# Fused set attention and gated convolution: token groups of 508 that carry their own halo, h summed over units on VectorE, and a last batch with float16 output products and a value product in two halves

## The chip, the core and the metric

The kernel runs on one core of one Trainium2 chip. The metric is the device time of one execution in microseconds; smaller is better. A core has TensorE (PE in the profile; PEld is its loading of weights), VectorE (DVE), ScalarE (ACT), GpSimd (POOL) and SyncE (SP), and 16 DMA engines that move data between main memory and the core's own.

## What is computed

For each of 4 batches, x holds 12800 tokens of 128 channels, and 32 inducing vectors of 128 channels are shared. The first attention makes h (32 by 128) from all tokens of the batch, the second attends from each token to h, and the result goes through a causal convolution over 5 tokens that gates a product with w_val, and a product with w_out:

```python
def mab(q, kv):
    s = scale * (q @ kv.transpose(0, 2, 1))
    a = softmax(s)
    return a @ kv
h = mab(inducing, x)
y = mab(x, h)
gate_pre[t] = sum(conv_w[k] * y[t - 4 + k] for k in range(5))
out = (sigmoid(gate_pre) * (y @ w_val)) @ w_out
```

h for a batch needs every token of that batch, so a batch has two stages with a short serial step between them.

## The kernel before

The tokens of a batch are cut into 7 **units**: 6 big ones of 4 groups with 512 tokens each, and a small one of 4 groups with 128 (`units`). The 4 groups of a unit lie in the 4 strips of 32 partitions, so that 32 score rows for each of 4 groups fill 128 partitions.

**Loads.** Each unit is loaded twice from main memory by SP's queue: `load_t` (L218) brings channels on partitions into tile xT (12 buffers), and `load_k` (L223) brings tokens on partitions into tile xk (4 buffers). The host lays xk out so that 128 consecutive tokens are the 128 rows of one block; a big unit has 16 blocks, and so 128 rows of 8 KB. SP issues the loads of all units in order, each xT followed by its xk, and waits at a load until its buffer is free.

**Stage 1**, per unit: scores in `a_mm` (L236), maximum in `a_max`, exponential in `a_exp`, transposes by PE in `a_tr` (L252), their copy in `a_ev`, and `a_h` (L265), which multiplies by xk and sums the unit's share of h; `a_hev` (L271) copies it to hs.

**Between the stages**, per batch: the functions `p_nl` to `p_we`. They find the maximum over the units and each unit's factor f, sum the 7 shares of h on PE (`p_h`, L321: 7 float32 products with a diagonal F made in `p_F`), and make the weights of stage 2: hq for the scores, and float16 high and low parts of the convolution and value weights (wstk). wo is w_out with a scale (L367).

**Stage 2**, per unit: scores `b_mm` (L389) from xT again, which is the last use of an xT buffer; a softmax in `b_tr` to `b_back`; float16 high and low parts in `b_hi` (L432, ACT) and `b_lo` (L437, POOL). The convolution needs the 4 tokens ahead of each group: `b_lo` copies them from the neighbouring group, or from the unit before (L442, L444: 4 small copies on POOL). Then `c_gate` (60 products, L453) fills 4 banks of tile g, `c_tanh` (L464, two halves) reads them, `c_val` (12 products, L453, tile v in the same 4 banks) starts when both halves are read, `c_gv` (L473, DVE) multiplies, `c_out` (L478) makes one float32 product for each group, `c_ev` (L485, ACT) copies it to tile os, and ACT issues the store (L487).

**Order.** A planner (`Plan.order`, L71) sets the order of all instructions on every engine while the program is built, from a duration and a key for each task; each engine then runs its list in that order. Stage 1 of a batch is interleaved with stage 2 of the batch before it; stage 2 of batch 3 runs alone at the end.

Of the kernel before, what the change touches and what calls it, by code (L numbers as in the profile page):

```python
# [18 lines left out]
P = 128  # L19
M = 32  # L20
# [4 lines left out]
SP = 16384.0  # L25
TINY = 1e-30


def units(b):
    small = [(0, 128)] if b == 0 else [(12288, 128)]  # L30
    big = [(2048 * u + 512 * (b == 0), 512) for u in range(6)]
    return small + big if b == 0 else big + small

# [4 lines left out]
BUFS = dict(xT=12, xk=4, E=2, ET=2, q=3, m=2, z=2, p=2, hl=3, gt=4, os=2, hs=1, nm=3, wst=2, wst2=2, gsc=2, hq=2, s=1, x=1, o=2, g=1)  # L38
LAT = 0.15
SLACK = 0.1  # L40
OUTK = 1.4
KA, KB, KP, KS = -2.5, 0.6, 4.0, 1.3
# [9 lines left out]

class Plan:
# [5 lines left out]
    def add(self, eng, dur, key, fn, args=(), deps=(), alloc=None, uses=(), lat=LAT):  # L59
        t = dict(i=len(self.tasks), eng=eng, dur=dur, key=key, fn=fn, args=args, deps=set(deps) | set(uses), alloc=alloc,  # L60
                 users=[], lat=lat, start=None, end=None)
# [71 lines left out]
def tile_kernel(ctx: ExitStack, tc: tile.TileContext, xT, xk, inducing, w_val, conv_w, w_out, out):  # L133
# [21 lines left out]
    def constants():  # L155
        warm = const.tile([P, 1], F32, name="warm")
        V.memset(warm, 0.0)
        S.activation(warm, warm, AF.Exp)
        ind = const.tile([M, P], F32, name="ind")
        nc.scalar.dma_start(ind, inducing)  # L160
        identf = const.tile([P, P], F32, name="identf")
        make_identity(nc, identf)
        ident = const.tile([P, P], F16, name="ident")
        V.tensor_copy(ident, identf)
        ones = const.tile([P, P], F32, name="ones")
        V.memset(ones, 1.0)
        id4 = const.tile([P, M], F32, name="id4")
# [50 lines left out]
    def load_t(b, u):  # L218
        t0, w = units(b)[u]
        x = st[b, u, "xT"] = sbt("xT", [P, G * 512])  # L220
        nc.sync.dma_start(x[:, :G * w], xT[b, :, t0:t0 + G * w])

    def load_k(b, u):  # L223
        t0, w = units(b)[u]
        n = G * w // P
        x = st[b, u, "xk"] = sbt("xk", [P, 16, P])
        nc.sync.dma_start(x[:, :n, :], xk[b, :, t0 // P:t0 // P + n, :])

    def a_mm(b, u):
        w = units(b)[u][1]  # L230
        if "nz" not in bat[b]:
            bat[b]["nz"] = sbt("nm", [P, 2, NU])
        sc = st[b, u, "s1"] = ps("s1", TAG1(b, u), [P, 512])
        x = st[b, u, "xT"]
        for g in range(G):
            T.matmul(sc[M * g:M * g + M, :w], c_["iw"], x[:, w * g:w * g + w], start=True, stop=True, tile_position=(0, M * g))  # L236
# [11 lines left out]
    def a_tr(b, u):  # L248
        w = units(b)[u][1]
        et = st[b, u, "etp"] = ps("et", "x", [P, 4, P])  # L250
        for i in range(w // P):
            T.transpose(et[:, i, :], st[b, u, "E"][:, P * i:P * i + P], c_["identf"])  # L252

    def a_ev(b, u):
        n = units(b)[u][1] // P
        et = st[b, u, "et"] = sbt("ET", [P, 4, P])
        S.copy(et[:, :n, :], st[b, u, "etp"][:, :n, :])  # L257

    def a_h(b, u):
        n = units(b)[u][1] // P  # L260
        hp = st[b, u, "h"] = ps("h", "x", [P, 512])
        et, x = st[b, u, "et"], st[b, u, "xk"]
        for i in range(n):
            for g in range(G):
                T.matmul(hp[M * g:M * g + M, :P], et[:, i, M * g:M * g + M], x[:, n * g + i, :],  # L265
                         start=i == 0, stop=i == n - 1, tile_position=(0, M * g))
# [37 lines left out]
    def p_F(b):  # L304
        d = bat[b]
        f = d["f"]
        F = d["F"] = sbt("F", [P, NU, M])
        V.tensor_tensor(F, c_["id4"].rearrange("p (o q) -> p o q", o=1).broadcast_to([P, NU, M]), f.broadcast_to([P, NU, M]), ALU.mult)
        zw = sbt("zw", [P, NU])
        V.tensor_tensor(zw, d["nz"][:, 1], f[:, :, 0], ALU.mult)  # L310
        zl = sbt("zl", [P, 1])
        V.tensor_reduce(zl, zw, AX.X, ALU.add)
        zf = d["zf"] = sbt("zf", [P, M])
        V.tensor_scalar(zf, c_["id4"], zl, None, ALU.mult)

    def p_h(b):
        d = bat[b]
        t = d["t"] = ps("t", TAGP(b), [P, 512])
        T.matmul(t[:, 256:256 + M], c_["ones"], d["zf"], start=True, stop=True)
        for u in range(NU):  # L320
            T.matmul(t[:, :M], d["hs"][:, u, :], d["F"][:, u, :], start=u == 0, stop=u == NU - 1)  # L321

# [15 lines left out]
    def p_w(b):  # L338
# [10 lines left out]
        V.tensor_scalar(vmx, vmx, TINY, 1.0 / SW, ALU.max, ALU.mult)  # L349
# [16 lines left out]
        wo = d["wo"] = sbt("wo", [P, P], tag="wst")  # L366
        V.tensor_scalar(wo, c_["w2"], vmx, 0.5 / SP, ALU.mult, ALU.mult)  # L367

# [15 lines left out]
    def b_mm(b, u):  # L384
        w = units(b)[u][1]
        sc = st[b, u, "s2"] = ps("s2", "s", [P, 512])
        x = st[b, u, "xT"]
        for g in range(G):
            T.matmul(sc[M * g:M * g + M, :w], bat[b]["hq"], x[:, w * g:w * g + w], start=True, stop=True, tile_position=(0, M * g))  # L389

    def b_tr(b, u):
        w = units(b)[u][1]
# [3 lines left out]
    def b_max(b, u):  # L396
        n = units(b)[u][1] // M
# [3 lines left out]
    def b_sub(b, u):  # L401
        n = units(b)[u][1] // M
# [3 lines left out]
    def b_exp(b, u):  # L406
        n = units(b)[u][1] // M
        q = st[b, u, "q"]
        S.activation(q[:, :n], q[:, :n], AF.Exp)  # L409

    def b_sum(b, u):
        n = units(b)[u][1] // M
        z = st[b, u, "z"] = sbt("z", [P, 16, 1])
        V.tensor_reduce(z[:, :n, 0], st[b, u, "q"][:, :n, :], AX.X, ALU.add)
        V.tensor_scalar(z[:, :n], z[:, :n], 1e-9, 1.0 / SP, ALU.add, ALU.mult)
        V.reciprocal(z[:, :n], z[:, :n])  # L416

    def b_norm(b, u):
        n = units(b)[u][1] // M
# [3 lines left out]
    def b_back(b, u):  # L423
        w = units(b)[u][1]
# [4 lines left out]
    def b_hi(b, u):  # L429
        w = units(b)[u][1]  # L430
        h = st[b, u, "hl"] = sbt("hl", [P, 2, 520], F16)
        S.copy(h[:, 0, 4:4 + w], st[b, u, "p"][:, :w])  # L432

    def b_lo(b, u):
        w = units(b)[u][1]
        h = st[b, u, "hl"]
        Gp.tensor_tensor(h[:, 1, 4:4 + w], st[b, u, "p"][:, :w], h[:, 0, 4:4 + w], ALU.subtract)  # L437
        if u == 0:
            Gp.memset(h[:M, :, 0:4], 0.0)
        else:  # L440
            v = units(b)[u - 1][1]
            Gp.tensor_copy(h[:M, :, 0:4], st[b, u - 1, "hl"][P - M:, :, v:4 + v])  # L442
        for g in range(1, G):
            Gp.tensor_copy(h[M * g:M * g + M, :, 0:4], h[M * g - M:M * g, :, w:4 + w])  # L444


    def strips(b, u, bank, d, k, first, last):
        w = units(b)[u][1]
        h, wst = st[b, u, "hl"], bat[b]["wst"]
        for i, (part, wp) in enumerate(((0, 0), (0, 1), (1, 0))):  # L450
            for g in range(G):
                s = slice(M * g, M * g + M)
                T.matmul(bank[:, g, :w], wst[s, wp, k, :], h[s, part, 4 - d:4 - d + w],  # L453
# [12 lines left out]
    def c_val(b, u):  # L466
        bank = st[b, u, "v"] = ps("v", "g", [P, G, 512])
        strips(b, u, bank, 0, TAPS, True, True)

    def c_gv(b, u, i):  # L470
        w = units(b)[u][1]
        t = st[b, u, i, "t"]
        V.scalar_tensor_tensor(t[:, :, :w], t[:, :, :w], 1.0, st[b, u, "v"][:, 2 * i:2 * i + 2, :w], ALU.add, ALU.mult)  # L473

    def c_out(b, u, g):
        w = units(b)[u][1]
        op = st[b, u, g, "o"] = ps("o", "o", [P, 512])
        T.matmul(op[:, :w], bat[b]["wo"], st[b, u, g // 2, "t"][:, g % 2, :w], start=True, stop=True)  # L478

    def c_ev(b, u, g):  # L480
# [4 lines left out]
        S.copy(os[:, w * g:w * g + w], st[b, u, g, "o"][:, :w])  # L485
# [16 lines left out]
    hl = {}  # L502
    hq = [None] * B
    ph = []
    wready = [None] * B

    def l(w, a, full):
        return a + (full - a) * w / 512

    def stage1(b):  # L510
# [23 lines left out]
        a = add("DVE", 1.05, k, p_F, (b,), deps=[a] + aexp)  # L534
        a = x = add("PE", 2.3, k, p_h, (b,), deps=[a] + hev, alloc=TAGP(b))
# [4 lines left out]
        a = add("DVE", 4.0, k, p_w, (b,), deps=[a, k2], uses=[x])  # L540
        for i in range(2):
# [5 lines left out]
    def stage2(b):  # L547
        nonlocal outs
        for u in range(NU):
# [11 lines left out]
            prev = [hl[b, u - 1]] if u else []  # L561
            lo = add("POOL", l(w, 1.05, 2.05), key, b_lo, (b, u), uses=[bk, hi] + [x[0] for x in prev], deps=[x[1] for x in prev])
            hl[b, u] = (hi, lo)
# [3 lines left out]
            va = add("PE", l(w, 0.19, 0.76), key - 0.3, c_val, (b, u), deps=th, uses=[hi], alloc="g")  # L567
# [4 lines left out]
            for i in range(2):  # L572
                gv = add("DVE", l(w, 0.15, 1.2), key - 0.5, c_gv, (b, u, i), uses=[th[i], va])
                for g in (2 * i, 2 * i + 1):
                    o = add("PE", l(w, 0.05, 0.92), key + OUTK, c_out, (b, u, g), deps=[gv], uses=[th[i]], alloc="o")
                    outs.append((o, g))
                    e = add("ACT", l(w, 0.1, 0.59) + (0.35 if g == 3 else 0.0), key + 0.9, c_ev, (b, u, g), uses=[o] + ([os] if g else []),
                            alloc=None if g else "os")
# [48 lines left out]
```

## Time and profile before

| | |
|---|---|
| median of the runs shown | 354.98 us (354.09 to 355.49, 3 runs) |
| profiled execution, its time and its span | 354.44 us, 352.7 us |
| PE, PEld busy | 315.0 us (89%), 139.3 us (39%) |
| DVE, ACT, POOL busy | 197.9 us (56%), 176.0 us (50%), 103.3 us (29%) |
| bytes moved, mean rate | 79.49 MB, 225 GB/s |

How to read it: a busy time is that of one engine over the span. The row PEclk is the granted clock of PE in tenths, DMA the mean busy share of the 16 DMA engines, each digit for one of 40 equal slices. A group row gives line, engine, operation, what is written <- what is read, its shape and count, then total and mean time and the idle time before it with what ended it. float32 products show two records for each instruction. The profile counts DMA packets for each queue: q1 is SP's, q10 ACT's.

### The profile page before, as it was taken

To read this page: it belongs to the slowest core of one execution; us is meant where nothing else is said; L and a number is where in the kernel's file an instruction comes from. 1 tells how busy PE (TensorE), PEld (TensorE's weight loads), DVE (VectorE), ACT (ScalarE), POOL (GpSimd) and SP (SyncE) were. 2 spreads that over 40 slices of the span, in tenths; PEclk is the share of its full clock that TensorE was granted. 3 is DMA by queue.
4 is the path that set the end of the run, shared out by engine and by line. 5 is a ranking of instruction groups with operands and counts; after the bars stand their busy time and mean duration, and the time that the engine had idled before them with its cause. 6 is when DMAs were issued, how large, how long until landed. Compare 5 with 4: busy or idle time off the path is not lost.

```text
span 352.7 us, 8776 instructions
## 1 busy us (share of the span) xinstructions
PE 315.0 (89%) x3722; PEld 139.3 (39%) x3722; DVE 197.9 (56%) x415; ACT 176.0 (50%) x314; POOL 103.3 (29%) x202
## 2 busy tenths in 40 slices
PE   2475698989999999999999999999999999887774
PEld 0333455543343454343353444443354333332332
DVE  1432356656579773664678563666667758722220
ACT  1223313556553647466553557465654555624443
POOL 0000003434531443144431123443451457721000
PEclk9989959999999999999999999999999999989999
DMA  7999999838983293698983394012223230232233
GB/s 306 419 419 413 419 415 421 315 159 326 388 360 121 70 391 120 227 336 302 414 354 123 106 390 164 32 62 103 93 106 122 121 124 26 119 121 121 119 121 150
DMA packets 12481, 79.49 MB, mean 225 GB/s; under 512 B 1397, under 2 KB 1690, under 8 KB 3226
## 3 DMA queue, kind: packets, MB, share of 16 engines
q1 hardware_dynamic: 8064, 52.43, 38.2%
q10 hardware_dynamic: 4378, 26.50, 18.4%
q8 instruction: 29, 0.48, 0.6%
q14 instruction: 10, 0.08, 0.1%
HBM read 52.71 MB, written 26.21 MB: 224 GB/s over the span
## 4 chain that ended last, share of the span: by engine, by line
PE 79%; ACT 7%; DMA 7%; DVE 5%; issue 1%; ACTq 0%; SPq 0%; DVEq 0%
PE o L478 25%; PE g L453 24%; PE s L389 7%; PE s L236 6%; PE h L265 6%; PE v L453 4%; DMA xT<-in_xt_dram 4%; PE et L252 3%; ACT gt L464 3%; DMA raw<-in_moe_w_out_dram 3%; DVE gt L473 2%; PE t L321 2%; ACT os L485 2%; ACT E L246 1%; DVE nm L240 1%
## 5 line engine op out<-in xcount | busy, mean ns | idle before, releaser
L478 PE MATMUL o<-gt,wo 128*128 128x512 f32 (+1 forms) x224 | 105.0, 584 | 9.1 <-DVE gt L473 8.5
L453 PE MATMUL g<-hl,wstk 32*128 32x512 f16 (+1 forms) x1680 | 86.3, 352 | 0.0
L485 ACT COPY os<-o 128x512 f32<-128x512 f32 (+1 forms) x112 | 58.9, 542 | 50.6 <-PE o L478 49.9
L473 DVE SCALAR_TENSOR_TENSOR gt<-gt,v 128x1024 f32<-128x1024 f32 (+1 forms) x56 | 59.5, 1103 | 41.8 <-ACT os L485 30.1
L453 PEld LDWEIGHTS <-wstk 32*128 32x128 f16 x2016 | 44.7, 92 | 75.2 <-issue 19.3
L464 ACT ACTIVATE gt<-g,gsc 128x1024 f32<-128x1024 f32 (+1 forms) x56 | 54.4, 1019 | 35.0 <-PE g L453 26.8
L478 PEld LDWEIGHTS o<-gt,wo 128*128 128x128 f32 x224 | 36.1, 190 | 53.0 <-issue 32.7
L404 POOL TENSOR_TENSOR q<-q,m 128x512 f32<-128x512 f32 (+1 forms) x28 | 26.7, 955 | 103.2 <-DVE m L399 102.3
L421 POOL TENSOR_TENSOR q<-q,z 128x512 f32<-128x512 f32 (+1 forms) x28 | 26.7, 954 | 70.0 <-DVE z L416 50.6
L437 POOL TENSOR_TENSOR hl<-p,hl 128x512 f16<-128x512 f32 (+1 forms) x28 | 29.6, 1057 | 39.0 <-ACT hl L432 38.8
L246 ACT ACTIVATE E<-s,nm 128x512 f32<-128x512 f32 (+1 forms) x28 | 18.0, 643 | 34.8 <-DVE nm L240 27.1
L265 PE MATMUL h<-xk,ET 128*32 128x128 f32 x800 | 29.7, 289 | 2.5 <-ACT ET L257 2.5
L236 PE MATMUL s<-xT,iw 128*32 128x512 f32 (+1 forms) x224 | 30.7, 624 | 0.6 <-DMA xT<-in_xt_dram 0.3
L240 DVE TENSOR_REDUCE nm<-s 128x1 f32<-128x512 f32 (+1 forms) x28 | 17.6, 630 | 24.3 <-PE s L236 24.1
L265 PEld LDWEIGHTS h<-xk,ET 128*32 128x32 f32 x800 | 23.0, 117 | 17.6 <-ACT ET L257 10.6
L252 PE MATMUL et<-identf,E 128*128 128x128 f32 x100 | 18.1, 303 | 12.8 <-ACT E L246 12.0
L432 ACT CAST hl<-p 128x512 f16<-128x512 f32 (+1 forms) x28 | 16.1, 575 | 26.4 <-DVE p L426 25.1
L389 PE MATMUL s<-xT,hq 128*32 128x512 f32 (+1 forms) x224 | 27.6, 562 | 1.0 <-DVE q L394 1.0
L394 DVE STREAM_TRANSPOSE q<-s 128x512 f32<-128x512 f32 (+1 forms) x28 | 18.1, 645 | 13.3 <-PE s L389 13.2
L426 DVE STREAM_TRANSPOSE p<-q 128x512 f32<-128x512 f32 (+1 forms) x28 | 17.9, 646 | 11.9 <-POOL q L421 10.7
L453 PE MATMUL v<-hl,wstk 32*128 32x512 f16 (+1 forms) x336 | 21.2, 354 | 1.9 <-ACT gt L464 1.9
L409 ACT ACTIVATE q<-q 128x512 f32<-128x512 f32 (+1 forms) x28 | 16.4, 589 | 13.0 <-POOL q L404 12.5
(85 smaller groups left out, 194.8 us busy)
## 6 DMA issues: line engine op xcount, KB each, us to landing
xT<-in_xt_dram SPq DMA_DIRECT2D x24, 1024.0 KB, 9.5
xk<-in_xk_dram SPq DMA_DIRECT2D x24, 1024.0 KB, 11.4
out_dram<-os ACTq DMA_DIRECT2D x24, 1024.0 KB, 4.5
xT<-in_xt_dram SPq DMA_DIRECT2D x4, 256.0 KB, 8.7
xk<-in_xk_dram SPq DMA_DIRECT2D x4, 256.0 KB, 6.3
out_dram<-os ACTq DMA_DIRECT2D x4, 256.0 KB, 2.0
raw<-in_moe_w_val_dram ACTq DMA_DIRECT2D x1, 128.0 KB, 7.6
raw<-in_moe_w_out_dram ACTq DMA_DIRECT2D x1, 128.0 KB, 10.1
```

What stands on the lines that cost most here:

```text
L236: T.matmul(sc[M * g:M * g + M, :w], c_["iw"], x[:, w * g:w * g + w], start=True, stop=True, tile_position=(0, M * g))
L252: T.transpose(et[:, i, :], st[b, u, "E"][:, P * i:P * i + P], c_["identf"])
L265: T.matmul(hp[M * g:M * g + M, :P], et[:, i, M * g:M * g + M], x[:, n * g + i, :], start=i == 0, stop=i == n - 1, tile_position=(0, M * g))
L389: T.matmul(sc[M * g:M * g + M, :w], bat[b]["hq"], x[:, w * g:w * g + w], start=True, stop=True, tile_position=(0, M * g))
L404: Gp.tensor_tensor(q[:, :n], q[:, :n], st[b, u, "m"][:, :n].broadcast_to([P, n, M]), ALU.subtract)
L421: Gp.tensor_tensor(q[:, :n], q[:, :n], st[b, u, "z"][:, :n].broadcast_to([P, n, M]), ALU.mult)
L437: Gp.tensor_tensor(h[:, 1, 4:4 + w], st[b, u, "p"][:, :w], h[:, 0, 4:4 + w], ALU.subtract)
L453: T.matmul(bank[:, g, :w], wst[s, wp, k, :], h[s, part, 4 - d:4 - d + w], start=first and i == 0, stop=last and i == 2, tile_position=(M * ...
L464: S.activation(t[:, :, :w], st[b, u, "g"][:, 2 * i:2 * i + 2, :w], AF.Tanh, scale=bat[b]["gsc"])
L473: V.scalar_tensor_tensor(t[:, :, :w], t[:, :, :w], 1.0, st[b, u, "v"][:, 2 * i:2 * i + 2, :w], ALU.add, ALU.mult)
L478: T.matmul(op[:, :w], bat[b]["wo"], st[b, u, g // 2, "t"][:, g % 2, :w], start=True, stop=True)
L485: S.copy(os[:, w * g:w * g + w], st[b, u, g, "o"][:, :w])
```

## The change

Big units get groups of 508 tokens and small ones groups of 152. A group's scores in stage 2 are made for 4 tokens (small: 8) more, those ahead of it, straight from xT, whose load brings 8 more tokens in front; main memory has 8 zero tokens ahead of each batch. So the 4 halo copies on POOL go. A block of xk has 127 tokens in big units and 76 in small ones, and `load_k` loads that many rows. xT has 11 buffers instead of 12.

h is summed over the units on VectorE (`p_hs`, 7 instructions in a row) and PE makes one product of the sum with id4 in place of 7 with F.

In every batch w_out's columns are scaled to a common size (`p_o1` to `p_o5`, with two transposes), and `c_ev` takes the scale off with a scale operand from SBUF. In batch 3, `c_out` works from float16 high and low parts of the gated value (`c_gh` on VectorE, `c_gl` on POOL) with three float16 products for each group; other batches keep the float32 product. In batch 3 `c_val` is issued in two halves of 2 groups, each behind its own half of the tanh; the value product now writes tile g itself.

The planner gets an offset for the key of some functions (a table KEYS), other durations and other constants. Of the diff, without the planner's table and durations:

```diff
-    small = [(0, 128)] if b == 0 else [(12288, 128)]
-    big = [(2048 * u + 512 * (b == 0), 512) for u in range(6)]
+    small = [(0, 152)] if b == 0 else [(12192, 152)]
+    big = [(2032 * u + 608 * (b == 0), 508) for u in range(6)]
...
+def block(w):
+    return 127 if w == 508 else 76
...
-BUFS = dict(xT=12, xk=4, E=2, ET=2, q=3, m=2, z=2, p=2, hl=3, gt=4, os=2, hs=1, nm=3, wst=2, wst2=2, gsc=2, hq=2, s=1, x=1, o=2, g=1)
+BUFS = dict(xT=11, xk=4, E=2, ET=2, q=3, m=2, z=2, p=2, hl=3, gt=4, os=2, hs=1, nm=3, wst2=2, gsc=2, osc=2, wh=2, wf32=2, gh=2, gl=2, hq=2, s=1, x=1, o=2, g=1)
...
     def load_t(b, u):
         t0, w = units(b)[u]
-        x = st[b, u, "xT"] = sbt("xT", [P, G * 512])
-        nc.sync.dma_start(x[:, :G * w], xT[b, :, t0:t0 + G * w])
+        x = st[b, u, "xT"] = sbt("xT", [P, 2048])
+        nc.sync.dma_start(x[:, :PAD + G * w], xT[b, :, t0:t0 + PAD + G * w])

     def load_k(b, u):
-        t0, w = units(b)[u]
-        n = G * w // P
+        w = units(b)[u][1]
+        k, n = block(w), G * w // block(w)
         x = st[b, u, "xk"] = sbt("xk", [P, 16, P])
-        nc.sync.dma_start(x[:, :n, :], xk[b, :, t0 // P:t0 // P + n, :])
+        nc.sync.dma_start(x[:k, :n, :], xk[b, :k, blocks(b, u):blocks(b, u) + n, :])
...
+    def p_hs(b, i):
+        d = bat[b]
+        u = (i + 1) % NU if b == 0 else i
+        if i == 0:
+            d["ha"] = sbt("ha", [P, P])
+            V.tensor_scalar(d["ha"], d["hs"][:, u, :], d["f"][:, u], None, ALU.mult)
+        else:
+            V.scalar_tensor_tensor(d["ha"], d["hs"][:, u, :], d["f"][:, u], d["ha"], ALU.mult, ALU.add)
...
-        for u in range(NU):
-            T.matmul(t[:, :M], d["hs"][:, u, :], d["F"][:, u, :], start=u == 0, stop=u == NU - 1)
+        T.matmul(t[:, :M], d["ha"], c_["id4"], start=True, stop=True)
...
-            Gp.tensor_copy(h[:M, :, 0:4], st[b, u - 1, "hl"][P - M:, :, v:4 + v])
-        for g in range(1, G):
-            Gp.tensor_copy(h[M * g:M * g + M, :, 0:4], h[M * g - M:M * g, :, w:4 + w])
...
+    def c_val(b, u, i):
+        n = NVAL(b)
+        strips(b, u, st[b, u, "g"], 0, TAPS, True, True, range(G // n * i, G // n * i + G // n))
...
+    def c_gh(b, u, i):
+        w = units(b)[u][1]
+        h = st[b, u, i, "gh"] = sbt("gh", [P, 2, 512], F16)
+        V.tensor_copy(h[:, :, :w], st[b, u, i, "t"][:, :, :w])
+
+    def c_gl(b, u, i):
+        w = units(b)[u][1]
+        l = st[b, u, i, "gl"] = sbt("gl", [P, 2, 512], F16)
+        Gp.tensor_tensor(l[:, :, :w], st[b, u, i, "t"][:, :, :w], st[b, u, i, "gh"][:, :, :w], ALU.subtract)
...
-        T.matmul(op[:, :w], bat[b]["wo"], st[b, u, g // 2, "t"][:, g % 2, :w], start=True, stop=True)
+        if not HALVES(b, g // 2):
+            T.matmul(op[:, :w], bat[b]["wf32"], st[b, u, g // 2, "t"][:, g % 2, :w], start=True, stop=True)
+            return
+        wh = bat[b]["wh"]
+        for i, (x, k) in enumerate((("gh", 0), ("gh", 1), ("gl", 0))):
+            T.matmul(op[:, :w], wh[:, k, :], st[b, u, g // 2, x][:, g % 2, :w], start=i == 0, stop=i == 2)
...
-        S.copy(os[:, w * g:w * g + w], st[b, u, g, "o"][:, :w])
+        S.activation(os[:, w * g:w * g + w], st[b, u, g, "o"][:, :w], AF.Copy, scale=bat[b]["osc"])
```

Three places in the built programs show what moves. The first is SP's list, its last two units; a row gives the line, the tile (numbers are buffers in the order of allocation), its source, and partitions x elements. Before:

```order
L221 DMA xT_2718<-in_xt_dram 128x2048
L227 DMA xk_2834<-in_xk_dram 128x2048
L221 DMA xT_2880<-in_xt_dram 128x512
L227 DMA xk_2889<-in_xk_dram 128x512
L623 UNCONDITIONAL_BRANCH
```

and after:

```order
L261 DMA xT_2695<-in_xt_dram 128x2040
L267 DMA xk_2724<-in_xk_dram 127x2048
L261 DMA xT_2870<-in_xt_dram 128x616
L267 DMA xk_2980<-in_xk_dram 76x1024
L735 UNCONDITIONAL_BRANCH
```

The order of the 56 loads stays; their shapes change, and those of xk have 127 and 76 rows.

The second place is PE's list around the last two products with xk (h is the share of h, o the output product, s2 the scores of stage 2, et the transposes, g the gate, v the value). Before:

```order
L265 MATMUL h_3206<-xk_2834,ET_3187 32x128 x16
L236 MATMUL s1_3227<-xT_2880,iw_89 32x128 x4
L478 MATMUL o_3239<-gt_3016,wo_2560 128x512
L478 MATMUL o_3241<-gt_3024,wo_2560 128x512
L478 MATMUL o_3252<-gt_3024,wo_2560 128x512
L252 MATMUL et_3257<-identf_71,E_3250 128x128
...
L265 MATMUL h_3334<-xk_2889,ET_3323 32x128 x4
L389 MATMUL s2_3341<-xT_1301,hq_2496 32x512 x4
L478 MATMUL o_3349<-gt_3174,wo_2560 128x512
L478 MATMUL o_3355<-gt_3174,wo_2560 128x512
```

and after:

```order
L308 MATMUL h_3180<-xk_2724,ET_3100 32x128 x16
L571 MATMUL o_3200<-gt_2817,wf32_1702 128x152
L474 MATMUL s2_3203<-xT_1506,hq_2500 32x512 x4
L293 MATMUL et_3212<-identf_71,E_3173 76x128 x2
L571 MATMUL o_3217<-gt_2996,wf32_2836 128x508
...
L308 MATMUL h_3242<-xk_2980,ET_3221 32x128 x8
L571 MATMUL o_3252<-gt_2996,wf32_2836 128x508
L571 MATMUL o_3256<-gt_3039,wf32_2836 128x508
L474 MATMUL s2_3261<-xT_1607,hq_2500 32x512 x4
```

In both, the work of stage 2 of batch 2 stands between the products with xk and behind them. In the new program 10 big gates, 2 small ones and one value product follow the last big product with xk.

The third place is PE's list over one unit of the last batch, from the end of one gate to the start of the next. Before:

```order
L453 MATMUL g_4359<-hl_4213,wstk_3779 128x512
L478 MATMUL o_4421<-gt_4324,wo_3701 128x512
L478 MATMUL o_4425<-gt_4324,wo_3701 128x512
L453 LDWEIGHTS wstk_3779
L453 MATMUL v_4430<-hl_4213,wstk_3779 128x512
...
L478 MATMUL o_4454<-gt_4423,wo_3701 128x512
L478 MATMUL o_4456<-gt_4423,wo_3701 128x512
L453 LDWEIGHTS wstk_3779
L453 MATMUL g_4460<-hl_4308,wstk_3779 128x512
```

and after:

```order
L533 MATMUL g_4315<-hl_4258,wstk_3645 128x508
L575 LDWEIGHTS wh_3776
L575 MATMUL o_4395<-gh_4311,wh_3776 128x508
...
L575 MATMUL o_4401<-gl_4379,wh_3776 128x508
L533 LDWEIGHTS wstk_3645
L533 MATMUL g_4315<-hl_4258,wstk_3645 128x508
...
L575 MATMUL o_4426<-gh_4377,wh_3776 128x508
...
L575 MATMUL o_4431<-gl_4405,wh_3776 128x508
L533 LDWEIGHTS wstk_3645
L533 MATMUL g_4441<-hl_4386,wstk_3645 128x508
```

Before, two of the four output products between two gates belong to the running unit (gt_4423 is made from v_4430) and two to the unit ahead of it. After, all four belong to the unit ahead, so that an output product never stands between a unit's gated value and the next gate.

More of the change, by code (lines that the diff above doesn't have):

```diff
@@ L249, in a_tr @@
         w = units(b)[u][1]
+        k = block(w)
         et = st[b, u, "etp"] = ps("et", "x", [P, 4, P])
-        for i in range(w // P):
-            T.transpose(et[:, i, :], st[b, u, "E"][:, P * i:P * i + P], c_["identf"])
+        for i in range(w // k):
+            T.transpose(et[:k, i, :], st[b, u, "E"][:, k * i:k * i + k], c_["identf"])
     def a_ev(b, u):
-        n = units(b)[u][1] // P
+        w = units(b)[u][1]
+        k, n = block(w), w // block(w)
         et = st[b, u, "et"] = sbt("ET", [P, 4, P])
-        S.copy(et[:, :n, :], st[b, u, "etp"][:, :n, :])
+        S.copy(et[:k, :n, :], st[b, u, "etp"][:k, :n, :])
     def a_h(b, u):
-        n = units(b)[u][1] // P
+        w = units(b)[u][1]
+        k, n = block(w), w // block(w)
         hp = st[b, u, "h"] = ps("h", "x", [P, 512])
@@ L401, in b_sub @@
     def b_sub(b, u):
-        n = units(b)[u][1] // M
+        n = wide(units(b)[u][1]) // M
         q = st[b, u, "q"]
@@ L406, in b_exp @@
     def b_exp(b, u):
[L407 removed]
+        n = wide(units(b)[u][1]) // M
         q = st[b, u, "q"]
```

162 lines of the change are left out of this document (111 added, 51 removed).

## The prediction, made before the changed kernel was run

> **What bounds the kernel now.** I read the page from the top, span and slices first, then the same by windows.
>
> ```profile
> span 352.7 us, 8776 instructions
> ...
> PE   2475698989999999999999999999999999887774
> ...
> DMA  7999999838983293698983394012223230232233
> GB/s 306 419 419 413 419 415 421 315 159 326 388 360 121 70 391 120 227 336 302 414 354 123 106 390 164 32 62 103 93 106 122 121 124 26 119 121 121 119 121 150
> ```
>
> There are three stages. In the first seven slices (to about 61 us) the DMA row is at 9 and PE is not: the loads set the pace. From there to slice 33 PE is full. In the last seven it falls to 7 or 8: batch 3 alone in stage 2, where a chain through several engines sets the pace. The same by windows; the last three numbers of a row are PE's granted clock, the share of the 16 DMA engines, and GB/s:
>
> ```profile
> 8.00:61.00 53.00, 37.15 (x508) 21.64 (x507) 23.79 (x71) 14.21 (x34) 2.61 (x8) 0.87 1.02 418
> 120.00:150.00 30.00, 30.00 (x390) 13.19 (x386) 16.24 (x28) 16.86 (x29) 8.88 (x15) 1.00 0.64 238
> 240.00:270.00 30.00, 30.00 (x294) 12.59 (x295) 22.47 (x53) 16.04 (x26) 10.12 (x23) 1.00 0.27 107
> ```
>
> With all 16 engines always busy they moved 418 GB/s, so one engine moves 418/16 = 26.1 KB per us. In the mixed window it is 238/(16 x 0.64) = 23.2 for the time that an engine was busy. Those two are my bounds for one engine's rate from rows. After 61 us the loads have slack, and SP waits for buffers, not for data:
>
> ```profile
> SPq L227 <- PE h L265: 81.6, 12, 23.8
> ```
>
> **The loads of xk, the term that decides.** The new `load_k` moves 127 rows of 8 KB in place of 128 (small units: 76 rows of 4 KB). That is less data. What matters is over how many of the 16 engines a transfer is divided, and the trace tells that by its packets:
>
> ```profile
> q1 hardware_dynamic: 8064, 52.43, 38.2%
> q10 hardware_dynamic: 4378, 26.50, 18.4%
> ```
>
> ```profile
> xT<-in_xt_dram SPq DMA_DIRECT2D x24, 1024.0 KB, 9.5
> xk<-in_xk_dram SPq DMA_DIRECT2D x24, 1024.0 KB, 11.4
> out_dram<-os ACTq DMA_DIRECT2D x24, 1024.0 KB, 4.5
> xT<-in_xt_dram SPq DMA_DIRECT2D x4, 256.0 KB, 8.7
> xk<-in_xk_dram SPq DMA_DIRECT2D x4, 256.0 KB, 6.3
> out_dram<-os ACTq DMA_DIRECT2D x4, 256.0 KB, 2.0
> raw<-in_moe_w_val_dram ACTq DMA_DIRECT2D x1, 128.0 KB, 7.6
> raw<-in_moe_w_out_dram ACTq DMA_DIRECT2D x1, 128.0 KB, 10.1
> ind<-in_inducing_dram ACTq DMA_DIRECT2D x1, 16.0 KB, 4.6
> raw<-in_moe_conv_w_dram ACTq DMA_DIRECT2D x1, 5.0 KB
> ```
>
> SP's 56 loads have 128 rows each: 8064/56 = 144 packets, one for each row and 16 more, one for each engine. On ACT's queue the 28 stores and two weight loads also have 128 rows: 30 x 144 = 4320. That leaves 58 for two transfers, one of 32 rows and one of 5: 32 + 16 = 48, and 5 + 5 = 10. So the 5 rows went to five engines, not 16, and in each transfer of the trace all shares are equal: 8 rows on each of 16, 2 on each of 16, 1 on each of 5. 127 has no divisor up to 16 but 1. If the shares must be equal, **all 127 rows go to one engine**; if they need not be, 16 engines take 8 rows and the last 7. No transfer of the trace has a row count that tells the two apart. I take equal shares, as all 88 transfers fit it, and price both.
>
> [...]
>
> With equal shares, one engine carries: 24 x 127 x 8192 B = 24.97 MB of xk; of the small xk loads (76 = 4 x 19 rows) 4 x 19 x 4096 B = 0.31 MB; its sixteenth of xT, (24 x 128 x 8160 + 4 x 128 x 2464)/16 B = 1.65 MB; and its sixteenth of the stores until the last load, about 14 units of 28, two batches of 0.41 MB, 0.82 MB. Together 27.75 MB. At 26.1 KB per us that is **1063 us**; at 23.2, 1196 us. One big xk takes 1.04 MB/26.1 = 40 us where the row above has 11.4 to landing. I take 26.1: it is from the window in which queues never emptied, and this engine's queue should not empty either. xk has four buffers and its next load needs only the product with the fourth load back, and a load of xT needs the scores of the unit 11 back; so one or two loads of 40 us each are always queued while PE does the work of a unit, some 10 us (the gates at 235.36 and 245.51 below). A load of xT has its share on the same engine behind them, so it lands late too, and every unit of both stages waits.
>
> **What comes after the last load.** In the new order of PE, 10 big gates and 2 small ones follow the last big product with xk. In the old trace those 12 gates run from here to the end:
>
> ```profile
> 232.39 2.93 PE L478 MATMUL o<-gt,wo 128*128 128x512 f32 x6
> 235.16 0.27 PE L252 MATMUL et<-identf,E 128*128 128x128 f32 x1
> 235.36 3.42 PE L453 MATMUL g<-hl,wstk 32*128 32x512 f16 x60
> 238.72 0.42 PE L265 MATMUL h<-xk,ET 128*32 128x128 f32 x8
> ...
> 241.84 0.83 PE L453 MATMUL v<-hl,wstk 32*128 32x512 f16 x12
> ...
> 244.51 1.07 PE L389 MATMUL s<-xT,hq 128*32 128x512 f32 x8
> 245.51 3.42 PE L453 MATMUL g<-hl,wstk 32*128 32x512 f16 x60
> ...
> 258.88 1.73 PE L321 MATMUL t<-F,hs 128*128 128x32 f32 x14
> ```
>
> 352.7 - 235.4 = 117.3 us, and ahead of them stand a value product (0.83), two sets of scores (2.1), three output products (2.9) and a transpose: 6.5, so 124 us. From that goes what the change takes off the last batch. One unit there, from the chain of waits (its first row here, the first scores of batch 3, is for a rival below):
>
> ```profile
> 264.44 1.00 PE s L389 x8
> ...
> 323.65 3.38 PE g L453 x60
> 327.06 2.12 ACT gt L464 x2
> 329.18 0.97 ACT os L485 x2
> 330.17 1.23 DVE gt L473
> 331.54 1.96 PE o L478 x4
> 333.50 3.38 PE g L453 x60
> ```
>
> The unit takes 9.85 us: gate, both halves of tanh, the value product (0.83, beside the two copies), one half of the gated value, two output products. After the change the first half of the value starts behind the first half of tanh: 1.06 + 0.42 + 1.23 for the first half of gv, then 1.23 for the second, on which the next gate waits; the output products stand elsewhere. So 3.38 + 3.94 and gaps of 0.1 at four hand-overs, 7.7 us; 2.2 less, for six units 13 us. Cover for the new work in 7.7 us: `c_gl` on POOL is twice the row below, 2.3 us a half and 4.6 a unit; `c_gh` on DVE goes by the cast of 768 columns, about 0.75 a half. Where they aren't hidden the last unit pays them, some 2 us. The last stage: 124 - 13 + 2 = **113 us**.
>
> ```profile
> L437 POOL TENSOR_TENSOR hl<-p,hl 128x512 f16<-128x512 f32 x24 | 27.9, 1162 | 28.9 <-ACT hl L432 28.9
> L362 DVE CAST wr<-wf 128x768 f16<-128x768 f32 x4 | 2.2, 560 | 0.1
> L444 POOL COPY hl<-hl 32x8 f16<-32x8 f16 x84 | 15.4, 183 | 4.9
> L271 DVE COPY hs<-h 128x128 f32<-128x128 f32 x28 | 7.9, 283 | 20.0 <-PE h L265 20.0
> L308 DVE TENSOR_TENSOR F<-id,f 128x224 f32<-128x224 f32 x4 | 1.9, 470 | 0.9 <-ACT f L302 0.8
> ```
>
> **The other edits.** They lie under the 40 us loads and I cost them at nothing there; their price without that cover is in the rival of 16 engines. The halo copies on POOL, 15.4 us and a few more, go; PE did not wait for them. Seven sums on VectorE, by the copy of 128 columns 7 x 0.28 = 2.0 us, for F's 0.47 are +1.5 us in the serial step; six of seven products fewer on PE take 1.73 x 6/7 = 1.5 us off it. The columns' scaling is some nine small VectorE instructions of about 0.2 us and two transposes a batch, not ahead of the first gate by PE's order. The scores of 4 more tokens a group make 512 columns, as before. `c_ev`'s scale operand costs ACT at most some 0.1 us for each copy (the tanh, which has one, takes 1.06 for 1024 columns, two copies 0.97), 4 a unit beside other work. One buffer fewer of xT matters where loads run ahead; here none do.
>
> **Sum**, against the profiled execution (354.44 us, 1.7 of it outside the span; the median of the runs is 354.98): 3 us to the first data, 1063, 113 and 1.7, together **1180 us**, over three times the time before.
>
> **The rivals.**
>
> *Sixteen engines share 127 rows unequally* (not slower). For it: nothing in the trace forbids it. Against it: no transfer there has unequal shares. Then the loads cost as before, and the rest counts: 354.4, less 11 for the last batch, and less some 4 for six products fewer in each of four serial steps (6 at most, nothing at least where the sums on VectorE are waited for): 339 us, 330 to 350. It decides when a load of 127 rows lands in some 10 us.
>
> *One engine, and its queue runs dry.* For it: SP issues in order, xT's buffers come free only by the next batch's scores, and these stand behind the serial step. In the old trace the last small product with xk of batch 3 is at 238.7 and the first scores of that batch at 264.4, 26 us. If three changes of batch expose this in full, 78 us more: 1260. Against it: the order leaves at least one big load queued there. A rate of 23.2 instead gives 1314.
>
> *A few engines, through some other split* (7 to 8, say): the stream shrinks to below the compute of 315 us of PE and the time is within some 10% of the old one. Nothing in the trace points to it.
>
> **How the numbers follow.** One engine, queue full: 0.75, 1180 us. One engine, dry or slow: 0.10, to 1314 and a little over. Sixteen: 0.13, 339. Other: 0.02. The range takes both one-engine cases, 0.85 in all, and leaves out the rest. Its upper end is the slow rate with a part of the dry spells, 1340. Below, a tenth for an engine that runs alone and may be quicker than one of sixteen (no row bounds that): 0.9 x 1063 + 118 = 1075. Within 0.5% is about what a measurement of this kernel can't tell from no change. Faster 0.12, same 0.01, slower 0.87.
>
> **What will show it.** Right: time from issue to landing of xk far above 40 us (loads queue), q1 with 24 x (127+1) + 4 x (76+4) + 28 x 144 = 7424 packets (7832 if sixteen engines share 127), DMA share near 1/16 to 2/16 for most of the span with about 70 GB/s, PE waiting for xk at the product with it, PE near a quarter busy, and a last stage of about 113 us with units of 7.7. Wrong: xk landing in 10 us; or a long stream whose rate is not near 26 KB per us.

## The result and the profile after

The changed kernel takes **1227.53 us** (median of 4 runs, 1224.38 to 1228.57), the kernel before 355.24 us beside it. The ratio is 3.452, 95% interval 3.436 to 3.469.

The page of the kernel after, the lines that answer to those shown of before:

```profile
span 1226.6 us, 8798 instructions
...
PE 360.3 (29%) x3746; PEld 153.3 (12%) x3746; DVE 227.7 (19%) x479; ACT 187.8 (15%) x314; POOL 111.9 (9%) x108
...
PE   1101110120200220172152320362332320359986
...
DMA  2011111111101110212211301221301301102222
GB/s 95 26 57 58 38 45 57 43 57 57 58 26 57 57 58 26 74 65 68 83 59 57 121 26 58 74 87 62 121 28 59 119 27 57 74 26 122 95 103 112
...
q1 hardware_dynamic: 7424, 52.55, 12.0%
q10 hardware_dynamic: 4378, 26.50, 5.2%
```

q1 has 7424 packets, the number forecast for one engine (7832 would have been sixteen). The row of GB/s has its floor at 26, in five slices of 31 us each (27 and 28 in two more): that is what one engine moves, and no slice lies below it. So one engine works all the time, and the rest is what xT and the stores add on the others. PE is busy for 29% of the span, and the DMA row stands mostly at 1 or 2.

The windows of the kernel after, for the stream and the last stage (columns as before: engine busy times with counts, then PE's granted clock, DMA share, GB/s):

```profile
100.00:1000.00 900.00, 209.91 (x2191) 91.33 (x2191) 127.86 (x292) 103.51 (x179) 49.50 (x52) 0.60 0.17 62
1100.00:1227.00 127.00, 108.52 (x1109) 41.65 (x1101) 79.57 (x140) 65.82 (x101) 56.82 (x46) 0.93 0.25 104
```

In the stream 62 GB/s; from 1100 us on PE is at work for 85% of the time. PE's granted clock in the stream is 0.60, which costs nothing there, since PE waits for the loads anyway.

The list of SP, which issues the loads, from the timeline of the kernel after (start, us, instruction):

```profile
65.77 2.85 SPq L267 DMA_DIRECT2D xk<-in_xk_dram  x1
68.66 39.81 SPq L261 DMA_DIRECT2D xT<-in_xt_dram  x1
108.52 2.83 SPq L267 DMA_DIRECT2D xk<-in_xk_dram  x1
111.39 39.69 SPq L261 DMA_DIRECT2D xT<-in_xt_dram  x1
...
237.54 2.92 SPq L267 DMA_DIRECT2D xk<-in_xk_dram  x1
```

Loads of xk follow each other at 42.9 us ((237.54 - 65.77)/4). In that time the one engine moves 127 rows of xk and its 8 rows of xT, 127 x 8192 + 8 x 8160 = 1.106 MB: 25.75 KB per us. The instruction that issues a load of xT itself lasts 40 us, where in the trace of before it lasts this (0.33 is also the median of its 28):

```profile
8.47 0.33 SPq L221 DMA_DIRECT2D xT<-in_xt_dram  x1
```

So SP is held while it issues, for about as long as the one engine needs for a load of xk (1.04 MB/25.75 = 40 us). What holds it, the trace does not show. The groups of PE that wait (last columns: idle time ahead of them and what ended it):

```profile
L276 PE MATMUL s<-xT,iw 128*32 128x508 f32 (+1 forms) x224 | 45.3, 897 | 671.2 <-DMA xT<-in_xt_dram 670.9
...
L308 PE MATMUL h<-xk,ET 127*32 127x128 f32 (+1 forms) x832 | 37.6, 336 | 110.2 <-DMA xk<-in_xk_dram 110.2
```

PE stands for 671 us at the scores, whose xT is one of the sixteen-engine loads, and for 110 us at the product with the slow xk: xT lands late too (its last load is issued from 1018.00 us on and its scores start at 1087.69, 69.7 us later, where the small loads of xT landed in 8.7 us before), and in PE's list the scores of a later unit stand ahead of the product. What delays it no run shows apart.

PE in the timeline of the kernel after, the last scores of stage 1, the last big product with xk and the gate behind it:

```profile
1087.69 0.74 PE L276 MATMUL s<-xT,iw 128*32 128x152 f32 x8 [34.33 <-DMA xT<-in_xt_dram]
...
1095.24 1.08 PE L308 MATMUL h<-xk,ET 127*32 127x128 f32 x32
...
1103.13 3.40 PE L533 MATMUL g<-hl,wstk 32*128 32x508 f16 x60
```

From the product to the end are 1226.6 - 1095.2 = 131 us. One unit of the last batch in the chain that ended last, kernel after:

```profile
1177.91 3.36 PE g L533 x60
1181.32 0.98 issue
1182.30 1.11 ACT gt L544
1184.37 1.23 DVE gt L554
1185.64 1.46 PE g L533 x6
1187.09 2.65 PE o L575 x6
1189.75 4.41 PE g L533 x59
```

and what the two halves of value waited for, in PE's timeline (in brackets the idle time and its releaser):

```profile
1183.45 0.82 PE L533 MATMUL g<-hl,wstk 32*128 32x508 f16 x6 [0.82 <-ACT gt L544]
1185.64 1.46 PE L533 MATMUL g<-hl,wstk 32*128 32x508 f16 x6 [1.37 <-DVE gt L554]
```

This unit takes 11.8 us, not the 9.85 of before, but part of that is PE's clock. The window of this unit, and that of the last big unit:

```profile
1177.80:1189.70 11.90, 9.71 (x89) 3.35 (x91) 6.63 (x11) 6.32 (x10) 7.75 (x6) 0.80 0.21 87
1202.40:1212.40 10.00, 7.75 (x89) 2.99 (x92) 4.78 (x4) 4.50 (x6) 3.82 (x2) 1.00 0.26 106
```

At a clock of 1.00 a unit takes 10.0 us. The first half of value starts at 1183.45, behind the *second* half of tanh (1182.30 + 1.11); the second starts behind the first half of the gated value (1184.37 + 1.23). The halves stand in a row. And each half takes 0.82 (the second 1.46 here, in a unit with a clock of 0.80), as the whole did before (0.83): its six products take the time of twelve. Ahead of the next gate stand output products of the unit ahead, 2.65 us here and 1.39 in the last big unit.

### The profile page after: what moved, and what is told of

Same layout as the page of the kernel before. It is cut to its first block, busy times and chain, and to the rows that moved or that the text cites. A ratio compares the mean times of both kernels' runs of the same rounds, so it can differ in the third digit from the quotient of the medians.

```text
span 1226.6 us, 8798 instructions
## 1 busy us (share of the span) xinstructions
PE 360.3 (29%) x3746; PEld 153.3 (12%) x3746; DVE 227.7 (19%) x479; ACT 187.8 (15%) x314; POOL 111.9 (9%) x108
## 3 DMA queue, kind: packets, MB, share of 16 engines
q1 hardware_dynamic: 7424, 52.55, 12.0%
## 4 chain that ended last, share of the span: by engine, by line
another core or an unknown queue 63%; PE 24%; DMA 8%; DVE 2%; ACT 2%; issue 1%; ACTq 0%; SPq 0%; DVEq 0%
PE g L533 8%; DMA xT<-in_xt_dram 8%; PE o L571 5%; PE s L276 3%; PE h L308 3%; PE s L474 2%; PE et L293 2%; PE o L575 1%; ACT gt L544 1%; DVE gt L554 1%; ACT os L582 0%; DVE nm L280 0%; ACT E L286 0%; PE wt L458 0%
## 5 line engine op out<-in xcount | busy, mean ns | idle before, releaser
L276 PE MATMUL s<-xT,iw 128*32 128x508 f32 (+1 forms) x224 | 45.3, 897 | 671.2 <-DMA xT<-in_xt_dram 670.9
L533 PE MATMUL g<-hl,wstk 32*128 32x508 f16 (+1 forms) x2016 | 120.2, 371 | 39.6 <-ACT gt L544 32.5
L582 ACT ACTIVATE os<-o,osc 128x508 f32<-128x508 f32 (+1 forms) x112 | 70.0, 642 | 180.5 <-PE o L571 127.4
L571 PE MATMUL o<-gt,wf 128*128 128x508 f32 (+1 forms) x168 | 88.9, 639 | 24.3 <-ACT os L582 24.2
L308 PE MATMUL h<-xk,ET 127*32 127x128 f32 (+1 forms) x832 | 37.6, 336 | 110.2 <-DMA xk<-in_xk_dram 110.2
L554 DVE SCALAR_TENSOR_TENSOR gt<-gt,g 128x1016 f32<-128x1016 f32 (+1 forms) x56 | 60.2, 1102 | 41.7 <-PE g L533 40.4
L544 ACT ACTIVATE gt<-g,gsc 128x1016 f32<-128x1016 f32 (+1 forms) x56 | 55.1, 1020 | 41.0 <-PE g L533 34.1
L308 PEld LDWEIGHTS h<-xk,ET 127*32 127x32 f32 (+1 forms) x832 | 29.6, 138 | 130.3 <-issue 122.6
L571 PEld LDWEIGHTS o<-gt,wf 128*128 128x128 f32 x168 | 30.3, 215 | 56.3 <-ACT os L582 32.7
L565 POOL TENSOR_TENSOR gl<-gt,gh 128x1016 f16<-128x1016 f32 (+1 forms) x14 | 27.8, 1992 | 32.0 <-DVE gh L560 30.6
```

What stands on the lines that cost most here:

```text
L276: T.matmul(sc[M * g:M * g + M, :w], c_["iw"], x[:, PAD + w * g:PAD + w * g + w], start=True, stop=True, tile_position=(0, M * g))
L308: T.matmul(hp[M * g:M * g + M, :P], et[:k, i, M * g:M * g + M], x[:k, n * g + i, :], start=i == 0, stop=i == n - 1, tile_position=(0, M * g))
L533: T.matmul(bank[:, g, :w], wst[s, wp, k, :], h[s, part, halo(w) - d:halo(w) - d + w], start=first and i == 0, stop=last and i == 2, tile_p ...
L544: S.activation(t[:, :, :w], st[b, u, "g"][:, 2 * i:2 * i + 2, :w], AF.Tanh, scale=bat[b]["gsc"])
L565: Gp.tensor_tensor(l[:, :, :w], st[b, u, i, "t"][:, :, :w], st[b, u, i, "gh"][:, :, :w], ALU.subtract)
L571: T.matmul(op[:, :w], bat[b]["wf32"], st[b, u, g // 2, "t"][:, g % 2, :w], start=True, stop=True)
```

## The experiments

Three questions: is it the 127 rows and their division over engines; what do the other parts of the change do without it; and why did pieces of xk that fit the theory not give the old time back. The theory is that of the prediction (equal shares, so one engine for 127 rows); the first rival, that something else in the change is slow.

**All 128 rows.** The row that no product reads is zeros.

```
-        nc.sync.dma_start(x[:k, :n, :], xk[b, :k, blocks(b, u):blocks(b, u) + n, :])
+        nc.sync.dma_start(x[:, :n, :], xk[b, :, blocks(b, u):blocks(b, u) + n, :])
```

> The kernel after, with one edit: a load of xk takes all 128 rows of the host's layout, the last one (for small units the last 52) being zeros that no product reads. Theory (equal shares over the largest divisor up to 16 of the row count, so 127 rows go to one engine): q1 shows 28 x (128+16) x 2 = 8064 packets again, the loads land as before the change, and all other parts of the change remain: about 339 us, 330 to 350. Rival (something else in the change is slow: products over 127 rows, loads of xT that start 8 columns ahead, the new order): the time stays over 1000 us.

Measured: 362.74 us, ratio to before 1.020 (1.013 to 1.026). Its page and, below, its loads:

```profile
q1 hardware_dynamic: 8064, 53.60, 38.5%
...
xk<-in_xk_dram SPq DMA_DIRECT2D x24, 1024.0 KB, 9.7
xT<-in_xt_dram SPq DMA_DIRECT2D x24, 1020.0 KB, 7.5
```

One row more in each big load, and 52 more in each small one, take 865 us off. The rival is out. But the rest of the change does not win 15 us, it loses 8; the forecast of 330 to 350 missed. Where, is seen from the first gate of the last batch. The chain of this version, that gate and the small one at its end:

```profile
283.98 3.36 PE g L533 x60
...
347.38 1.13 PE g L533 x60
```

and the same two gates in the chain of before:

```profile
281.27 3.35 PE g L453 x60
...
343.34 0.95 PE g L453 x60
```

To the end are 361.5 - 284.0 = 77.5 us, before 352.7 - 281.3 = 71.4. Of the 9 us between the two spans 6 arise here. The six units take 63.4 us, 10.6 each, and before 62.1, 10.3 each: that is 1 us of the 6. The other 5 lie behind the small gate, where 14.1 us follow in place of 9.4.

**127 rows in the kernel before.**

```
-        nc.sync.dma_start(x[:, :n, :], xk[b, :, t0 // P:t0 // P + n, :])
+        for lo, hi in ((0, 127), (127, 128)):
+            nc.sync.dma_start(x[lo:hi, :n, :], xk[b, lo:hi, t0 // P:t0 // P + n, :])
```

> The kernel before, with one edit: each load of xk is two, of 127 rows and of 1 row. Nothing else of the change. Theory: 127 rows and the single row each go to one engine, which carries 25.17 + 1.05 MB of xk, 1.64 of xT and 0.82 of stores, 28.7 MB at the 25.65 KB per us of the kernel after: 1118 us, and with 124 us behind the last load about 1245 us (1210 to 1290); q1 shows 28 x 144 + 28 x (128 + 2) = 7672 packets. Rival (the slowness comes from another part of the change): about 355 to 360 us. Rival (127 rows over sixteen engines unequally): 355, and q1 with 28 x 144 + 28 x (143 + 2) = 8092 packets.

Measured: 1241.25 us, ratio 3.504 (3.480 to 3.527). Its page:

```profile
q1 hardware_dynamic: 7672, 52.43, 11.7%
```

The row count alone, put into the old kernel, makes the whole slowdown, within 1% of the sum, and the packets are those of one engine.

**Other divisors.** Two runs of the changed kernel with xk in two pieces, 112 + 15 rows and 125 + 2 rows (the small units 64 + 12):

```
-        nc.sync.dma_start(x[:k, :n, :], xk[b, :k, blocks(b, u):blocks(b, u) + n, :])
+        for lo, hi in ((0, 112), (112, 127)) if k == 127 else ((0, 64), (64, 76)):
+            nc.sync.dma_start(x[lo:hi, :n, :], xk[b, lo:hi, blocks(b, u):blocks(b, u) + n, :])
```

> The kernel after, with each big load of xk split into 112 and 15 rows and each small one into 64 and 12: still exactly the bytes that the changed kernel needs. Theory: 112 = 16 x 7 goes to sixteen engines, 15 to fifteen, 64 to sixteen, 12 to twelve; q1 shows 28 x 144 + 24 x (128 + 30) + 4 x (80 + 24) = 8240 packets, and the time is that of the 128-row version within 2%. Rival (only counts that are multiples of 8 or 16 are spread, others go to one engine): the 15 rows, 123 KB, go to one engine, 4.7 us each at 26 KB per us, beside 2.2 us for its seven rows of the 112 and 2.5 of xT: that engine paces the first 13 loads or so, some 9 us a unit in place of 5, 20 to 40 us more than the 128-row version; packets 28 x 144 + 24 x (128 + 16) + 4 x (80 + 13) = 7860.

> The kernel after, with each big load of xk split into 125 and 2 rows (125 = 5 x 25; small ones 64 and 12). Theory: 125 rows go to five engines, 25 each, 205 KB or 8.0 us at 25.65 KB per us, beside 2.5 us for their share of a load of xT; so the first batches' loads take 10.5 to 11 us a unit in place of 5, while the whole stream of an engine is 24 x 0.205 + 1.65 + 0.8 = 7.4 MB, 288 us, and the work behind the last load some 110 us: 375 to 400 us; q1 shows 28 x 144 + 24 x (130 + 4) + 4 x (80 + 24) = 7664 packets. Rival (odd counts go to one engine): about 1200 us. Rival (any count spreads over sixteen unequally): the time of the 128-row version.

Measured: 395.82 us (ratio 1.113, 1.104 to 1.122) and 490.04 us (1.383, 1.372 to 1.395). Page, then window, of 112 + 15:

```profile
q1 hardware_dynamic: 8240, 52.55, 46.9%
```

```profile
8.00:61.00 53.00, 32.02 (x308) 17.95 (x304) 17.38 (x55) 10.66 (x25) 0.00 (x0) 0.75 1.02 289
```

and of 125 + 2:

```profile
q1 hardware_dynamic: 7664, 52.55, 35.1%
```

```profile
8.00:61.00 53.00, 19.33 (x180) 10.19 (x177) 8.72 (x21) 5.45 (x12) 0.00 (x0) 0.81 0.61 172
```

Both packet counts are those of the theory: 15 rows on fifteen engines, 125 on five. So the counts bear it out, while both times miss. For 125 + 2 part of it was my sum: I put the whole stream at 288 us and 110 behind it, but SP's last load goes out at 338.5 us, 12.1 us a unit over all 28, and 152 us follow; what the excess of 12.1 over the forecast 10.5 to 11 comes from stays open. At 112 + 15 the time, 33 us over the 128-row version, is the one that the rival gave (20 to 40). But the rival lets one engine pace the others, and its packets would be 7860; here all engines are busy (1.02), yet they move 289 GB/s where before they moved 418 at the same share. Each packet takes longer, 0.35 us of an engine's time over the run (46.9% of 16 x 389.3 us for 8240) against 0.27 before (38.2% of 16 x 352.7 us for 8064), and that needs another cause.

**Which partitions.** A load of xk in the kernel before writes all 128 partitions, and a piece of it only some; does it matter which? Two runs of the kernel *before*, both with 8512 packets on q1 and the same bytes, xk in two transfers of 64 rows: halves, and even and odd rows.

```
+        for r in (slice(0, 64), slice(64, 128)):
+            nc.sync.dma_start(x[r, :n, :], xk[b, r, t0 // P:t0 // P + n, :])
```

```
+        for r in (slice(0, 128, 2), slice(1, 128, 2)):
+            nc.sync.dma_start(x[r, :n, :], xk[b, r, t0 // P:t0 // P + n, :])
```

> The kernel before, each load of xk as two of 64 rows, the first half of the partitions and the second. [...] Rival (each transfer costs something by itself, however its rows lie): as much as in the run with even and odd rows.

> The kernel before, each load of xk as two of 64 rows, the even partitions and the odd ones. The same number of transfers, packets and bytes as the run with two halves; only which partitions one of them writes differs. Theory (which partitions count): both spread over all partitions, so 410 to 418 GB/s and 354 to 359 us. Rival (each transfer costs by itself): the time of the run with two halves.

Measured: halves 400.38 us (ratio 1.128, 1.120 to 1.137), even and odd 355.71 us (0.995, 0.990 to 1.000). The windows, halves first:

```profile
8.00:61.00 53.00, 26.66 (x271) 13.31 (x267) 11.42 (x29) 8.90 (x21) 0.00 (x0) 0.77 1.03 261
```

```profile
8.00:61.00 53.00, 38.78 (x435) 22.27 (x435) 22.65 (x69) 13.69 (x33) 1.26 (x4) 0.81 1.02 417
```

With all engines busy in both, 261 GB/s against 417: twice as many transfers cost nothing in the second, and in the first, with 64 neighbouring partitions for each transfer, the rate is 37% lower. The time went up by 45 us; from the 289 GB/s of 112 + 15 rows I had estimated 20 to 30. Whether 112 + 15 rows are slow for this reason (its second piece lies in 15 neighbouring partitions) was not tried by itself and stays open.

**The last batch.** Two runs on the 128-row version: its new form undone, and gate and value in two tiles of two banks.

```
-    return 2 if b == 3 else 1
+    return 1
...
-    return b == 3
+    return False
```

> The 128-row version, with the last part of the change undone: value in one piece and float32 output products in all batches, as in the first three. Theory (all of the 8 us by which the 128-row version is slower than the kernel before lies in the last batch, whose units became longer): 354 to 357 us, the stretch from the first gate of the last batch to the end 71 to 72 us in place of 77.5. Rival (the loss lies in the other parts: longer small units, products for columns' scaling, the new order): 360 to 364.

```
-        bank = st[b, u, "g"] = ps("g", "g", [P, G, 512])
+        bank = st[b, u, "g"] = [ps("g0", "g0", [P, 2, 512]), ps("g1", "g1", [P, 2, 512])]
...
-                T.matmul(bank[:, g, :w], wst[s, wp, k, :], h[s, part, halo(w) - d:halo(w) - d + w],
+                T.matmul(bank[g // 2][:, g % 2, :w], wst[s, wp, k, :], h[s, part, halo(w) - d:halo(w) - d + w],
```

> The 128-row version of the changed kernel (362.7 us), with one edit: the four banks of gate and value are two tiles of two banks in place of one tile. Nothing is computed otherwise. Theory: in the last batch the two halves of value stand in a row only because they share a tile (the first half of value waits for both halves of tanh, the second half of value for the first half of the gated value); with two tiles the gate of 3.36, the output products of the unit before beside the tanh (1.4 to 1.5), value 0.82, twice 1.22 and gaps come to 8.5 us a unit in place of 10.5 (63.4 us from the first to the seventh gate of the last batch, six units): 10 to 13 us less, 350 to 353 us. Rival (PE, not the chain of waits, sets the unit: 3.36 for the gate, two halves of value at 0.82 each, 2.8 to 4.1 of output products and scores): less than 4 us gained, 359 to 363.

Measured: undone 353.00 us, ratio 0.9947 (0.9912 to 0.9982), so all other edits together win 2 us (0.6 to 3.1), and the last batch's new form loses 9 to 10. With two tiles 345.63 us, ratio 0.974 (0.969 to 0.978): 17 us below the one-tile version and faster than both kernels. PE's timeline of the two-tile version, two units:

```profile
306.57 3.75 PE L533 MATMUL g<-hl,wstk 32*128 32x508 f16 x60
311.70 1.76 PE L533 MATMUL g<-hl,wstk 32*128 32x508 f16 x12
314.89 3.52 PE L533 MATMUL g<-hl,wstk 32*128 32x508 f16 x60
319.74 1.62 PE L533 MATMUL g<-hl,wstk 32*128 32x508 f16 x12
322.68 3.76 PE L533 MATMUL g<-hl,wstk 32*128 32x508 f16 x60
```

A unit takes 8.1 us ((322.68 - 306.57)/2), and both halves of value run through without a wait. In the last batch PE's list is the same in both versions, so the order is no rival. The theory holds: the shared tile put the halves in a row. The gain was larger than forecast, 17 us against 10 to 13.

**Float16 halves elsewhere, or nowhere.** On the two-tile version, `HALVES` true in all batches, in 1 to 3, in 2 and 3, and in none (one line each: `return True`, `return b >= 1`, `return b >= 2`, `return False`).

> The version with 128 rows and two tiles (345.6 us), with output from float16 halves in all four batches in place of the last. Theory (PE, busy 91% of the span, sets the pace before the last batch): two outputs take 1.39 us of PE in place of 1.90, 0.25 each, for 84 outputs of three batches 21 us less: 325 to 332 us. Rival (the halves load DVE with 0.77 and POOL with 2.3 us a half unit, 28 and 85 us more in those batches, and PE waits for them at the output products or at the next gate): 338 to 350, PE's share of the span falling under 88%.

> The same with the halves in batches 1, 2 and 3. Theory (PE sets the pace): 14 us less than with the last batch alone, 331 to 336. Rival (DVE or POOL): 338 to 350.

> The same with the halves in batches 2 and 3. Theory (PE sets the pace): 7 us less than with the last batch alone, 337 to 341. Rival (DVE or POOL): 342 to 350.

> The version with 128 rows and two tiles (345.6 us), with float32 output products in the last batch too, so that no float16 halves are made; the value still comes in two halves there. Theory (with two tiles PE sets the unit of 8.2 us, and four float32 outputs take 3.8 us of it in place of 2.8): 1.0 us a unit more for six units, 350 to 352 us. Rival (making the halves holds DVE and POOL up for as much as PE saves): 343 to 347.

Measured: 367.64 (ratio 1.040, 1.032 to 1.047), 360.50 (1.019, 1.011 to 1.027), 359.12 (1.014, 1.007 to 1.021) and, for none, 346.52 (0.977, 0.972 to 0.982), which can't be told from the 0.974 of the last batch alone. For three the sign is the rival's, and they are slower than even it said; the last agrees with it. The window of a full stretch with halves everywhere:

```profile
180.00:240.00 60.00, 53.86 (x689) 23.21 (x689) 53.79 (x106) 33.87 (x61) 38.05 (x30) 0.94 0.63 232
```

and of the two-tile version:

```profile
180.00:240.00 60.00, 59.06 (x789) 26.53 (x792) 41.46 (x94) 33.59 (x60) 15.74 (x16) 1.00 0.47 179
```

VectorE goes from 41 to 54 us of 60, and PE falls from 59 to 54 with a granted clock of 0.94. Part of VectorE's time is the same instructions lasting longer. Its group at L500, first in the two-tile version (mean 313 ns), then with halves everywhere (806):

```profile
L500 DVE SCALAR_TENSOR_TENSOR z<-z,eps 128x16 f32<-128x16 f32 (+1 forms) x28 | 8.8, 313 | 1.0
```

```profile
L500 DVE SCALAR_TENSOR_TENSOR z<-z,eps 128x16 f32<-128x16 f32 (+1 forms) x28 | 22.6, 806 | 1.0
```

One of these in the timeline with halves everywhere:

```profile
200.35 2.11 POOL L565 TENSOR_TENSOR gl<-gt,gh 128x1016 f16<-128x1016 f32 x1 [1.93 <-DVE gh L560]
200.45 2.03 DVE L500 SCALAR_TENSOR_TENSOR z<-z,eps 128x5 f32<-128x5 f32 x1
```

Five columns on VectorE end at 202.48, as POOL's `c_gl` ends at 202.46. How much of the loss comes with such longer instructions and how much with VectorE's own new work was not told apart.

## Why the prediction was right, and where it was not

1. **127 rows on one engine: right.** The packets of four kernels (7424, 7672, 8240, 7664) are those of equal shares over the largest divisor up to 16. One more row takes 865 us off; the same split in the kernel before puts them on.
2. **The stream, 1063 us and 3 ahead: mechanism right, 29 us short.** The last big product came at 1095, not 1066. The rate was 25.75 KB per us, not 26.1: 27.75 MB/25.75 = 1078, 15 us of it. Another 7.5 are PE's list: the last scores start at 1087.7, when the load of xT issued behind the last big xk has landed, and output products, transposes and a gate (4.28) stand between them and the product. The remaining 6 or 7 are not placed. The queue did not run dry: in stretches of 6 us from 10 to 1090 us the rate never falls below 25 GB/s.
3. **PE waits at the product with xk: mostly wrong, and without effect on the time.** It waited 671 us at the scores and 110 at the product. That xT lands late behind xk was in the text, but not that PE meets it first.
4. **The last stage, 113 us: 18 us short, with a change of the wrong sign.** I took 13 us off for units of 7.7; measured 131. Up to the first gate of the last batch it went as forecast (52 us, and 124 - 71.4 = 52.6). Six units from 1147.3 to 1212.4 take 65, 10.8 each, where before they took 62 and the sum left 49; behind them come 14.2 us in place of 9.4, where I had allowed 2 more for the halves. The step that failed is "1.06 + 0.42 + 1.23 for the first half of gv": it let the first half of value start behind the first half of tanh, and priced it at half of 0.83. In this program the halves share a tile, and half the products take the whole 0.82. So the second tanh (1.11), the other half of 0.82 and the second value (0.82) join the chain: 2.3 us more, which makes the 10.0 of a unit at a clock of 1.00. The rest of the 10.8 comes with lower clocks: three of the six units, at 0.78 to 0.86, take 11.5 to 12.7. The two-tile version, where the halves do run apart, has units of 8.1.
5. **"The other edits" at nothing: right.** Under the loads they cannot be seen, and with 128 rows, with the last batch undone, they win 2 us of 355, which is within 2%.
6. **The rival of sixteen engines, 339 us (330 to 350): wrong by the same step as 4.** With 128 rows, which stand in for it, it is 362.7; with the step put right by two tiles 345.6.

The errors in 2 and 4 are 29 and 18 us in the same direction, together the 47 us between 1180 and 1227.5; the range, made for the engine's rate and for dry spells, covered both. That it covered the second was luck: no part of it was meant for the last stage.

## What to carry to other kernels

When a tile's partition count changes, look first at the number of rows in its transfers, and then at which partitions one transfer spans; here 127 in place of 128 cost 865 us, a hundred times the 8 of the other edits, and a padded row (362.7 us) was cheaper than both splits of the 127 (395.8 and 490.0). Here a chain that was cut in halves gained only once each half had its own tile (362.7 to 345.6 us); look in the trace for what each half waits for. Before moving work from a full engine, price it on the engine that takes it, with what becomes slower there: here the group at L500 went from 8.8 to 22.6 us.

## What the runs showed of the hardware that was not expected

- The instruction that issues a load can itself be held: 39 to 45 us for 18 of the 28 loads of xT among the one-engine loads, 0.33 in the median before. What stands behind it on SP waits too: the hold from 25.54 us on lasts 40.19, and the next load goes out at 65.77.
- Six products at two of the four row positions take 0.82 us, twelve at four take 0.83, at the full clock.
- A small VectorE instruction of two operands (median 0.18 us in the two-tile version) lasted 2.03 us beside a 2.11 us subtraction on POOL. The two ended within 0.02 us of each other; no run here took the one away alone.
- PE's granted clock was lower in stretches where PE waits: 0.60 in the stream, 0.94 with halves everywhere, 1.00 in the full stretch of the two-tile version. But it doesn't follow the waiting alone: two units of the last batch, with PE busy for about 80% of each, had 0.80 and 1.00.
